# Moving the first spectral piece of a step into the second half of gate and up, and the sigmoids behind the second piece

## The chip, the cores and the metric

The kernel runs on one core of a Trainium2 chip. The metric is the device time of one execution in microseconds (us). The profile is that of one execution; L followed by a number is a source line of the kernel that was profiled.

## The reference

Forward and backward of a gated mix: a spectral branch (2-D FFT, a product with learned weights, inverse FFT) and a GeGLU feed-forward branch. Eight results are wanted: the output and the gradients of everything but `B_x`.

```python
def _A_ref(x, w_r, w_i):
    X = rfft2(x.astype(float32)) * (w_r + 1j * w_i)
    return irfft2(X, s=(S, D)).astype(bfloat16)
def _B_ref(x, w_gate, w_up, w_down):
    return (gelu(x @ w_gate) * (x @ w_up)) @ w_down
g = sigmoid((A_x * gate_w).sum(-1, keepdims=True))
out = g * _A_ref(...) + (1 - g) * _B_ref(...)
# S = 2048 tokens, D = 576, F = 4608; then the vector-Jacobian product with grad_out
```

## The kernel before

After a head of some 51 us there are 72 steps: 18 groups `g` of 256 hidden columns, each with 4 blocks `m` of 512 tokens. I number the steps 0 to 71, so step 37 is g = 9, m = 1. A step computes z (the gradient through w_down) and gate and up for its tokens on TensorE, in two halves of two token tiles; ScalarE takes each half out of PSUM, the memory that the matmuls write (q, xb, hu); VectorE and two sigmoids (om, s) make the tiles A, dHg, dHu. Behind that, TensorE runs weight-gradient units (dwd, dw) of the group before. The FFTs are cut into pieces (pf) and put between these as fillers: in steps 0 to 9 the forward pieces (Y, V), to about step 45 the middle ones (64-partition ones of L659, and L748), then the inverse ones (Z, U, D) to step 64. After the loop come dense matmuls.

The order of a step in the source:

```python
z, xy_full = H_mm(g, m)
xy = xy_full(0)                  # 8 matmuls of 512 columns
da = H_da(m, z)                  # ScalarE empties z
H_act(0, xy, tiles, 0); ...; H_act(0, xy, tiles, 1)     # q, then xb and hu
def second():
    xy = xy_full(1)              # 8 matmuls
    if g == 0:
        fft_next()               # one spectral piece: its matmuls, then its copy by ScalarE
    for part in range(2):
        H_act(1, xy, tiles, part)
    state.append(H_ew1(tiles)); side_work(1.4)
...
second()
at, k, late = 0.0, 0, [sigs]     # at: us of weight-gradient work so far
for w, f in carry + hs:          # halves of dwd (w 1.0) and dw (w 1.7) units
    if k < n and at >= (0.0, 1.0, 3.6, 5.0)[k]:
        fft_next(); k += 1
    if late and at >= 1.6 and k >= min(n, 2):
        late.pop()()             # the sigmoids, then VectorE's eight products
    f(); at += w
```

The PSUM tiles that matter:

```python
ph = tile_pool(name="ph", bufs=2, space=PSUM)    # the two halves of gate and up
pz = tile_pool(name="pz", bufs=1, space=PSUM)    # z AND every spectral piece, one buffer
pw = tile_pool(name="pw", bufs=2, space=PSUM)    # weight gradients (wps), two buffers
```

Each unit's second half ends with its eviction by ScalarE (`wevac`). The units of a group are spread over the blocks: m = 1 has three dwd units (I call it a d step), the other blocks have one or two units of dw, tails or dwd.

## Time and profile before

| | before |
|---|---|
| time, median of 3 | 1480.13 us |
| TensorE busy | 1391.3 us, 94% |
| ScalarE, VectorE busy | 722.1 us (49%), 732.4 us (50%) |
| granted TensorE clock | 0.994 |
| one period of four steps (37 to 40) | 54.08 us |

The period is read between the starts of z. The first and the last of them, from the TensorE timeline of before (columns: start, duration, engine, line, operation, out<-in, shape, count):

```profile
548.08 1.91 PE L380 MATMUL z<-wdT,dOT 128*128 128x256 bf16 x16
...
602.16 1.58 PE L380 MATMUL z<-wdT,dOT 128*128 128x256 bf16 x13
```

602.16 - 548.08 = 54.08. Busy time says little here: a matmul's row is longer than its distance to the next (z: 276 ns on average, 109 ns from start to start). I therefore work with starts: where nothing holds TensorE up, matmuls of 128, 256, 288 and 512 columns start 56, 109, 122 and 216 ns apart in this trace (medians), which N/2.4 + 2.5 ns for N columns fits, and what goes beyond that is lost. Summed this way from the trace, TensorE loses 28.5 us in steps 0 to 9, 49.3 in steps 10 to 44 and 28.6 in steps 45 to 70. Not all of that is waiting: the profiles of before and after lack the record of one gate-and-up matmul per step (1080 of 1152 are there; in experiments 1 to 7 all are), and the sum counts its 0.216 us as lost. Without that it is about 26.3, 41.7 and 23.0 us.

### The profile page before, as it was taken

Reading aid. Unit: us, or ns where it says so; the run is one execution under the profiler, and the core shown is the slowest. Engines: PE = TensorE matmul, PEld = TensorE weight load, DVE = VectorE, ACT = ScalarE, POOL = GpSimd, SP = SyncE. Lnnn points to the kernel's source line nnn. Section 1 sums busy time; section 2 is a strip of 40 time slices with the busy share of each in tenths; the row PEclk is TensorE's granted clock in tenths of the full one; section 3 lists DMA queues with packets and bytes.
Section 4 is the critical chain, followed back from the end, with each engine's and each line's share of the span. In section 5 each row is a group of like instructions: output and inputs, shape, how many; then the busy total and the mean of one; then the engine's idle time right before and its main releaser. Section 6 shows DMA issues by size and latency. Waiting matters only on the chain.

```text
span 1478.9 us, 28110 instructions
## 1 busy us (share of the span) xinstructions
PE 1391.3 (94%) x11342; PEld 1024.0 (69%) x11414; DVE 732.4 (50%) x1394; ACT 722.1 (49%) x1311; POOL 125.7 (8%) x230
## 2 busy tenths in 40 slices
PE   6888898999999999999999999999999999999998
PEld 4555665666666666666676666677877777777776
DVE  6575546767766766755655655653000471212111
ACT  5676777677677677666776666664000000000000
POOL 3000010010010011000001001000000110000000
PEclk9999999999999999999999999999999999999999
DMA  5233354444544543454445436666999997787873
GB/s 187 79 115 106 115 141 122 128 131 128 158 115 117 156 132 112 126 154 113 120 134 158 133 108 153 161 154 144 255 184 189 222 228 162 164 160 163 157 154 75
DMA packets 516477, 214.96 MB, mean 145 GB/s; under 512 B 312921, under 2 KB 510554, under 8 KB 516346
## 3 DMA queue, kind: packets, MB, share of 16 engines
q1 hardware_dynamic: 506714, 192.65, 56.0%
q0 software_dynamic: 7824, 19.49, 4.4%
q8 instruction: 89, 1.46, 0.4%
q10 hardware_dynamic: 1808, 1.02, 0.3%
q14 instruction: 42, 0.34, 0.1%
HBM read 40.76 MB, written 93.84 MB: 91 GB/s over the span
## 4 chain that ended last, share of the span: by engine, by line
PE 80%; ACT 10%; DVE 4%; issue 3%; DMA 1%; SPq 0%; POOL 0%; ACTq 0%; DVEq 0%; POOLq 0%
PE acc L1092 28%; PE xy L392 15%; PE wps L495 12%; PE wps L478 8%; PE z L380 8%; PE wps L508 2%; PE xy L387 2%; ACT hu L412 2%; ACT xb L411 2%; PE z L383 1%; ACT q L409 1%; ACT Vt L751 1%; ACT om L433 1%; ACT Xx L664 1%; ACT Xg L664 1%
## 5 line engine op out<-in xcount | busy, mean ns | idle before, releaser
L1092 PEld LDWEIGHTS <-pin 128*128 128x128 bf16 x3456 | 337.7, 98 | 87.8 <-DMA pin<-scr 2.5
L392 PE MATMUL xy<-wgu,xT 128*128 128x512 bf16 x1080 | 247.6, 379 | 10.2 <-issue 9.5
L495 PEld LDWEIGHTS <-xn 128*128 128x128 bf16 x2304 | 224.3, 98 | 29.6 <-issue 0.2
L392 PEld LDWEIGHTS <-xT 128*128 128x128 bf16 x1152 | 106.8, 98 | 148.8 <-issue 30.6
L402 ACT ACTIVATE da<-z,omg 128x256 bf16<-128x256 f32 x288 | 112.8, 474 | 121.8 <-PE z L383 121.8
L1109 ACT COPY bo<-acc 128x288 f32<-128x288 f32 x32 | 12.7, 398 | 306.8 <-PE acc L1092 282.2
L380 PE MATMUL z<-wdT,dOT 128*128 128x256 bf16 x1152 | 140.6, 276 | 13.5 <-ACT Y L556 5.2
L478 PE MATMUL wps<-dB,A 128*128 128x288 bf16 x1152 | 150.8, 286 | 0.0
L1092 PE MATMUL acc<-wd_all,pin 128*128 128x288 bf16 x1152 | 142.9, 286 | 1.3 <-DMA pin<-scr 1.3
L1092 PE MATMUL acc<-wuT,pin 128*128 128x288 bf16 x1152 | 143.6, 286 | 0.3 <-DMA pin<-scr 0.3
L1092 PE MATMUL acc<-wgT,pin 128*128 128x288 bf16 x1152 | 143.8, 286 | 0.0
L495 PE MATMUL wps<-dHg,xn 128*128 128x256 bf16 x1152 | 136.2, 272 | 0.0
L380 PEld LDWEIGHTS <-dOT 128*128 128x128 bf16 x1152 | 112.9, 99 | 33.5 <-issue 18.3
L438 DVE TENSOR_TENSOR xb<-xb,s 128x1024 bf16<-128x1024 bf16 x72 | 49.8, 692 | 172.7 <-ACT s L434 172.7
L495 PE MATMUL wps<-dHu,xn 128*128 128x256 bf16 x1152 | 134.6, 272 | 0.0
L478 PEld LDWEIGHTS <-A 128*128 128x128 bf16 x1152 | 112.2, 98 | 28.0
L409 ACT ACTIVATE q<-xy 128x512 bf16<-128x512 f32 x144 | 86.0, 597 | 61.0 <-PE xy L392 61.0
L501 POOL DMA_DIRECT2D out_dram<-dw x67 | 48.8, 728 | 658.8 <-ACT dw L456 535.2
L417 DVE TENSOR_SCALAR s<-q 128x1024 bf16<-128x1024 bf16 x72 | 30.7, 426 | 146.0 <-ACT q L409 145.9
L1169 DVE SCALAR_TENSOR_TENSOR f32t<-gwf,dlog,b16t 128x576 f32<-128x576 f32 x16 | 13.1, 818 | 170.6 <-DMA b16t<-dxa_scr 170.6
L412 ACT CAST hu<-xy 128x512 bf16<-128x512 f32 x144 | 87.1, 605 | 0.0
L411 ACT CAST xb<-xy 128x512 bf16<-128x512 f32 x144 | 83.6, 580 | 0.0
(197 smaller groups left out, 1594.5 us busy)
## 6 DMA issues: line engine op xcount, KB each, us to landing
scr<-A SPq DMA_DIRECT2D x72, 256.0 KB, 2.5
scr<-dHg SPq DMA_DIRECT2D x72, 256.0 KB, 2.6
scr<-dHu SPq DMA_DIRECT2D x72, 256.0 KB, 3.0
out_dram<-dw POOLq DMA_DIRECT2D x67, 128.0 KB, 2.3
wd_all<-in_B_w_down_dram SPq DMA_DIRECT2D x3, 1728.0 KB, 14.8
out_dram<-dwd POOLq DMA_DIRECT2D x34, 144.0 KB, 2.8
scr_p<-Vt SPq DMA_DIRECT2D x32, 145.0 KB, 2.4
wgu<-in_B_w_gate_dram SPq DMA_DIRECT2D x18, 256.0 KB, 3.3
```

Source lines behind the costliest of these rows:

```text
L380: nc.tensor.matmul(zo(t), lhsT=dOT[:, ci, t, :], rhs=wdT[:, ci, :], start=(t % 4 < 2 and ci == 0), stop=False)
L392: nc.tensor.matmul(xy[k][:, t % 2, :], lhsT=xT[:, ci, t, :], rhs=wgu[:, ci, :], start=False, stop=(ci == 3))
L402: nc.scalar.activation(da[:, t, :], z[:, t % 2, t // 2, :], ACT.Copy, scale=omg32[:, 4 * m + t:4 * m + t + 1])
L409: nc.scalar.activation(q[:, h, :], xy[:, :, 0:FG], ACT.Square)
L411: nc.scalar.copy(xb[:, h, :], xy[:, :, 0:FG])
L412: nc.scalar.copy(hu[:, h, :], xy[:, :, FG:2 * FG])
L417: V.tensor_scalar(s[:], q[:], A_GELU, 1.0, op0=ALU.mult, op1=ALU.add)
L438: V.tensor_tensor(xb[:], xb[:], s[:], op=ALU.mult)
L478: nc.tensor.matmul(wps[:, :288], lhsT=tl(0, t)[:, fch * P:(fch + 1) * P], rhs=dB[:, t, h * 288:(h + 1) * 288], start=(t == 0), stop=(t == ...
L495: nc.tensor.matmul(wps[:, cc, :], lhsT=xn[:, t, (c0 + cc) * P:(c0 + cc + 1) * P], rhs=tl(k, t), start=(t == 0), stop=(t == T - 1))
L501: wst[0].dma_start(ov[:, c0:c0 + TPB, fsl], dw[:])
L1092: nc.tensor.matmul(acc[:, :288], lhsT=src[:, r, :], rhs=w_of(r)[:, h * 288:(h + 1) * 288], start=(first and r == 0), stop=(last and r == F ...
```

## The change

In the code, `n` is the number of spectral pieces that the schedule gives to a step, `k` how many of them have been placed, and `between` is called in the middle of a half, between its two token tiles. The intent: let the first piece's copy run while TensorE still works on the second half, so that the single pz buffer is free when the second piece comes, and start the sigmoids earlier.

```diff
-        def full(k):
+        def full(k, between=None):
             for t in ts[2 * k:2 * k + 2]:
+                if t % 2 and between:
+                    between()
                 for ci in range(4):
                     nc.tensor.matmul(...)
@@ spectral schedule
-        out = [first] + [gap] * 5
+        out = [first] + [gap] * 7
-    mid_at = 2 * T + 8
+    mid_at = 2 * T + 10
@@ second()
-                xy = xy_full(1)
-                if g == 0:
-                    fft_next()
+                xy = xy_full(1, fft_next if n or g == 0 else None)
@@ the loop over weight-gradient work
-                at, k, late = 0.0, 0, [sigs]
+                at, k, late = 0.0, min(n, 1), [sigs]
-                    if k < n and at >= (0.0, 1.0, 3.6, 5.0)[k]:
+                    if k < n and at >= (0.0, 1.0, 3.0, 5.0)[k]:
-                    if late and at >= 1.6 and k >= min(n, 2):
+                    if late and at >= 1.0:
```

## The prediction

> **What bounds the kernel now.** I read the page first, then who waited for whom on TensorE, then the timelines of TensorE and ScalarE for one period of four steps, because order inside a step is all the change touches.
>
> ```profile
> PE 1391.3 (94%) x11342; PEld 1024.0 (69%) x11414; DVE 732.4 (50%) x1394; ACT 722.1 (49%) x1311; POOL 125.7 (8%) x230
> ```
>
> TensorE is the bound, ScalarE and VectorE are half idle, so only TensorE's gaps can be won. Among its waits the largest are of this kind (columns: waiter, releaser, us in total, times, longest):
>
> ```profile
> PE pf L659 <- ACT Xx L664: 7.6, 8, 1.0
> PE pf L659 <- ACT Vt L751: 6.8, 6, 1.1
> PE pf L748 <- ACT Xg L664: 6.7, 7, 1.0
> ...
> PE z L380 <- ACT ZT L797: 2.2, 2, 1.1
> ```
>
> All spectral pieces (pf) and the step's z use one two-bank PSUM tile, so a piece waits for the copy of the piece before. Now the TensorE timeline from a step with 48 dwd matmuls (call it the d step) into the next:
>
> ```profile
> 554.14 0.41 PE L748 MATMUL pf<-qn,BTtab 128*128 128x290 bf16 x2
> 554.39 1.14 PE L478 MATMUL wps<-dB,A 128*128 128x288 bf16 x8
> 556.67 0.41 PE L659 MATMUL pf<-Vp,Btab 128*128 128x289 bf16 x2 [1.14 <-ACT Vt L751]
> 556.92 5.06 PE L478 MATMUL wps<-dB,A 128*128 128x288 bf16 x40
> 561.82 1.91 PE L380 MATMUL z<-wdT,dOT 128*128 128x256 bf16 x16
> ...
> 567.88 0.41 PE L659 MATMUL pf<-Vp,Btab 128*128 128x289 bf16 x2
> 568.13 1.91 PE L495 MATMUL wps<-dHg,xn 128*128 128x256 bf16 x16
> 570.99 0.41 PE L659 MATMUL pf<-Vp,Btab 128*128 128x289 bf16 x2 [0.95 <-ACT Xx L664]
> ```
>
> and ScalarE in the d step:
>
> ```profile
> 552.61 0.60 ACT L409 ACTIVATE q<-xy 128x512 bf16<-128x512 f32 x1 [0.69 <-PE xy L392]
> ...
> 555.30 0.60 ACT L412 CAST hu<-xy 128x512 bf16<-128x512 f32 x1
> 555.77 0.85 ACT L751 CAST Vt<-pf 128x580 bf16<-128x580 f32 x1
> 557.12 1.28 ACT L664 CAST Xx<-pf 64x578 bf16<-64x578 f32 x2 [0.49 <-PE pf L659]
> 558.42 0.40 ACT L456 CAST dwd<-wps 128x288 bf16<-128x288 f32 x1
> 558.72 1.06 ACT L433 ACTIVATE om<-s 128x1024 bf16<-128x1024 bf16 x1
> 559.81 1.06 ACT L434 ACTIVATE s<-s 128x1024 bf16<-128x1024 bf16 x1
> ```
>
> The first piece's copy stands behind all six copies of gate and up; ScalarE reaches it at 555.77 although its matmuls began at 554.14. The second piece waits it out. Lost time, start to start: 40 dwd matmuls fill 556.92 to 561.82, 0.1225 us each; eight after 554.39 end at 555.37, so the piece at 556.67 is 1.30 late. In the next step 16 matmuls of 256 columns end at 568.13 + 16 x 0.109 = 569.88 (0.109: sixteen z matmuls take 1.91, the last of them 0.27, so 1.64 over 15), so 570.99 is 1.11 late. The period's other two steps lose 1.11 and 0.54 likewise.
>
> **What the Trainium skill says.** "Perfetto Trace Analysis", section Optimization Strategy: a gap that repeats on the engine that should be full can mean that no buffer is free for the next tile. The trace agrees: 1.11 and 1.30 recur every four steps. "TensorE: Matmul & The Clock Gate", section Architectural detail, has ScalarE's queue as strictly first in first out while TensorE may only pull weight loads ahead; the copy at 555.77 behind hu shows the first half. The same page, Back-to-back issue gap, gives columns/2.4 + 2.5 ns, 109 ns for 256, which is what I measure. And "Perfetto Trace Analysis", section Matmuls, wants independent groups to rotate through PSUM banks so evacuation hides; wps has two buffers and does, pf has one and doesn't.
>
> **The change, part by part.** It adds and removes no work. In a step with pieces, the first goes between the two token tiles of the second half, its copy ahead of that half's q, xb, hu; the third piece comes a bit earlier; two empty slots shift the middle stage; the sigmoids follow the second piece at once. The built order of the new kernel confirms this, and shows one more move: in the d step ScalarE had copy, copy, dwd, om, s, dwd, dwd; now it has copy, (q xb hu), copy, om, s, dwd, dwd, dwd. The first dwd eviction has fallen behind both sigmoids.
>
> I write X for the first q of a step (552.61 above), when the second half's matmuls start. Spacings on ScalarE from the trace: q to xb 0.49, xb to hu 0.47, hu to next 0.48; Vt to next 0.70; the pair of Xx copies 1.19; om to s 1.09; s to eviction 0.97. The first piece now runs at X+0.85 and its copy at X+1.44 (hu of the first half starts at X+0.96). The second half ends on TensorE at X+1.96.
>
> *Step with two 64-partition pieces (the one at 566.35).* Copy 1.44 to 2.73, so the second piece, due at 1.96 + 1.745 = 3.70, no longer waits: the 1.11 goes. q 2.63, hu 3.59, second copy 4.14, om 5.33, s 6.42, dw 7.39. TensorE ends with 3.95 + 1.745 + 1.96 = X+7.65, against 8.59 (574.94 - 566.35): gain 0.94. *Next step*: 3.95 + 1.745 + 3.49 = 9.19 against 10.12, gain 0.93. *Next*: 7.65 against 8.01, gain 0.36.
>
> *The d step.* Copy 1.44 to 2.29, q 2.14, hu 3.10, second piece at 2.94 without waiting, its copy 3.58 to 4.87, om 4.77, s 5.86, first dwd 6.83 to 7.23. But dwd units rotate through the two wps buffers, and the third takes the first's buffer. It is due at 2.94 + 0.25 + 24 x 0.1225 = 6.13 and must wait until 7.23 + 0.05 (the release at 556.67 came 0.05 after the copy's end). It ends at 7.28 + 16 x 0.1225 = 9.24, against 9.21 before: the 1.30 is replaced by 1.15 and the gain is nil.
>
> So a period gains 0.94 + 0.93 + 0.36 - 0.03 = 2.20 instead of the 4.06 it loses. There are seven periods in the middle stage (the steps from 208.9 to 602 us, 30 of them): 15.4. At its edges: a third piece put into its first step costs 0.6 at the end but spares 0.25 before it; the d step with one piece now stalls 0.64; the two last steps with four short pieces win back 1.07. Middle: about 15.5.
>
> *Inverse stage (20 steps, 664 to 945 us).* The same reckoning with copies of 1.02 (ZT), 0.37 (ZU), 0.66 (ev). Start-to-start losses at pieces and at z after one are some 14 us. The d steps here go well: one with four pieces has first dwd evicted by 6.5 and the third unit due at 6.7. Where the fourth piece ends a step, z still waits for its copy: 0.6 to 1.3 in six steps, as before, but in other steps. Step by step the sum of gains is 9.2, less 1.8 for three d steps that have no first piece but whose dwd eviction also falls behind the sigmoids (0.56, 0.56, 0.67: third unit due at X+5.55, released at 6.11). Net 7.4.
>
> *Forward stage (first ten steps, 51 to 184 us).* In the first four the piece waits for VectorE, whose Vt sums stand behind the elementwise chain, and now four matmuls of the half queue behind that waiting piece: q comes 0.33 later in three steps, 0.55 earlier in the first. Steps five to ten gain 0.85, 0.71, 0.15, 0.13, -0.2, 0.12. Net 1.3.
>
> Everything after about 1010 us (dense matmuls, 98% busy) is untouched. Sum 15.5 + 7.4 + 1.3 = 24.2 us, 1480.1 - 24.2 = 1456.
>
> **Rivals.** *A, all pf waits vanish and nothing replaces them.* For: ScalarE is 49% busy, and the middle stage loses 32 us start to start (7 x 4.06 and the edges). Then 32 + 9 + 1 = 42 us, 1438, over 2% faster. Against: the dwd eviction order above, and nobody hides a copy that ends a step. *B, the new wps wait is worse than I reckon*, for instance because om also waits for VectorE's s (q delayed by 0.4, then tensor_scalar and product), or because a delayed q makes VectorE late for the A, dHg, dHu tiles. VectorE waits up to 5.9 us for the sigmoids, so it has room; s is ready at X+4.0, before om's turn at 4.77. If every d step lost 1 us more, 17 us of the gain would go: 1473. *C, forward steps become slower*, since a waiting piece in the middle of a half blocks four matmuls (0.86 us) and delays q. At worst 0.5 in four steps: +2 us, and a slip into half clock such as the trace shows at 85 us (z took 3.31 instead of 1.91) may add 1.4.
>
> **Range and chances.** Durations and orders are measured, the addition is mine; the most doubtful are the inverse stage (plus or minus 4) and the d steps (plus or minus 5). Range 1447 to 1468. Over 2% faster means under 1450.5, 6 us beyond my centre: 0.2. Within 2%: 0.78. Slower by over 2%: 0.02.
>
> **What would show it.** Right: waits of pf on Xx, Vt and Xg (some 24 us in the list above with their kin) nearly gone; a new wait of PE wps L480 for ACT dwd, about 1.1 us, in each d step; steps of 12.2, 13.7, 12.2 and 13.8 us in a period instead of 13.1, 14.7, 12.6 and 13.7; busy times unchanged. Wrong: no such wps wait (rival A), waits of the moved piece itself on hu or da, or gaps before z in the middle stage.

## The result

| | before | after |
|---|---|---|
| median of 4 runs | 1478.66 us (1477.17 to 1481.99) | 1459.97 us (1457.31 to 1461.30) |
| profiled span | 1478.9 us | 1457.1 us |

The ratio is 0.9868, with a 95% interval from 0.9843 to 0.9893: 1.3% faster, inside the predicted range of 1447 to 1468 and within 2%.

The page's first line after, then the longest waits of TensorE after (waiter, releaser, us in total, times, longest):

```profile
PE 1386.9 (95%) x11342; PEld 1023.7 (70%) x11414; DVE 731.4 (50%) x1394; ACT 715.5 (49%) x1311; POOL 125.6 (9%) x230
```

```profile
PE wps L480 <- ACT dwd L458: 10.7, 13, 1.3
...
PE pf L568 <- DVE Vt L575: 5.7, 4, 2.0
...
PE pf L661 <- ACT Vt L753: 2.2, 1, 2.2
```

The 24.5 us of middle pieces waiting for copies of Xx, Vt and Xg (7.6, 6.8 and 6.7 in the prediction's list, and 3.4 of L748 for Vt) have shrunk to single cases, and a wait that before did not have has taken the first place: dwd matmuls wait for the eviction of an earlier dwd, 13 times. The third line is one single wait of 2.2 us, to which experiment 6 returns.

The d step after (step 37) and the next one, from the TensorE timeline:

```profile
541.70 0.41 PE L750 MATMUL pf<-qn,BTtab 128*128 128x290 bf16 x2
541.95 1.02 PE L394 MATMUL xy<-wgu,xT 128*128 128x512 bf16 x4
542.81 1.14 PE L480 MATMUL wps<-dB,A 128*128 128x288 bf16 x8
543.79 0.41 PE L661 MATMUL pf<-Vp,Btab 128*128 128x289 bf16 x2
544.04 3.10 PE L480 MATMUL wps<-dB,A 128*128 128x288 bf16 x24
548.41 2.12 PE L480 MATMUL wps<-dB,A 128*128 128x288 bf16 x16 [1.27 <-ACT dwd L458]
...
558.43 0.41 PE L661 MATMUL pf<-Vp,Btab 128*128 128x289 bf16 x2
```

and ScalarE in the same d step:

```profile
541.04 0.60 ACT L411 ACTIVATE q<-xy 128x512 bf16<-128x512 f32 x1 [0.69 <-PE xy L394]
...
542.47 0.85 ACT L753 CAST Vt<-pf 128x580 bf16<-128x580 f32 x1
543.15 0.64 ACT L411 ACTIVATE q<-xy 128x512 bf16<-128x512 f32 x1
...
544.57 1.33 ACT L666 CAST Xx<-pf 64x578 bf16<-64x578 f32 x2
545.80 1.05 ACT L435 ACTIVATE om<-s 128x1024 bf16<-128x1024 bf16 x1
546.89 1.06 ACT L436 ACTIVATE s<-s 128x1024 bf16<-128x1024 bf16 x1
547.97 0.70 ACT L458 CAST dwd<-wps 128x288 bf16<-128x288 f32 x2
```

The first piece stands between two groups of gate-and-up matmuls, and its copy (542.47) ahead of the second q (543.15). Neither this d step's second piece (543.79) nor the next step's (558.43) waits any more. But the first dwd eviction now follows om and s. It starts at 547.97; the third dwd unit, which needs its buffer, could have started at 544.04 + 24 x 0.1225 = 546.98 and starts at 548.41, 1.43 late.

Lengths of steps 37 to 40, between the starts of z:

| step | before | predicted | after | experiment 1 |
|---|---|---|---|---|
| 37 (d step) | 13.74 | 13.77 | 13.87 | 12.44 |
| 38 | 13.13 | 12.18 | 12.01 | 12.01 |
| 39 | 14.67 | 13.72 | 13.56 | 13.56 |
| 40 | 12.55 | 12.18 | 12.02 | 12.01 |

The predicted column is the end of each step after X, as the prediction has it, plus 4.53 us from z to X (552.61 - 548.08). Over the whole kernel, by stages between starts of z:

| stretch | before | after | gain | predicted |
|---|---|---|---|---|
| head, to step 0 | 50.8 | 49.8 | 0.9 | 0 |
| steps 0 to 9 | 133.3 | 135.5 | -2.2 | 1.3 |
| steps 10 to 44 | 468.4 | 452.9 | 15.6 | 15.5 |
| steps 45 to 70 | 352.5 | 345.3 | 7.2 | 7.4 |
| rest | 474.0 | 473.6 | 0.3 | 0 |

The change does not touch the head, so its 0.9 shows how far two executions scatter.

### The profile page after: what moved, and what is told of

The parts are those of the page before. It is cut to its first block, busy times and chain, and to the rows that moved or that the text cites. A ratio compares the mean times of both kernels' runs of the same rounds, so it can differ in the third digit from the quotient of the medians.

```text
span 1457.1 us, 28112 instructions
## 1 busy us (share of the span) xinstructions
PE 1386.9 (95%) x11342; PEld 1023.7 (70%) x11414; DVE 731.4 (50%) x1394; ACT 715.5 (49%) x1311; POOL 125.6 (9%) x230
## 3 DMA queue, kind: packets, MB, share of 16 engines
q10 hardware_dynamic: 1808, 1.02, 0.2%
## 4 chain that ended last, share of the span: by engine, by line
PE 82%; ACT 9%; DVE 3%; issue 3%; SPq 1%; DMA 1%; POOL 0%; ACTq 0%; DVEq 0%; POOLq 0%
PE acc L1092 28%; PE wps L497 16%; PE xy L394 14%; PE z L380 8%; PE wps L480 7%; PE xy L387 2%; PE wps L510 2%; PE z L383 1%; ACT om L435 1%; ACT xb L413 1%; ACT hu L414 1%; ACT q L411 1%; DMA pin<-scr 1%; ACT Xx L666 1%; ACT s L436 1%
## 5 line engine op out<-in xcount | busy, mean ns | idle before, releaser
L394 PE MATMUL xy<-wgu,xT 128*128 128x512 bf16 x1080 | 258.8, 380 | 10.1 <-issue 9.4
L480 PE MATMUL wps<-dB,A 128*128 128x288 bf16 x1152 | 153.8, 288 | 10.7 <-ACT dwd L458 10.7
L440 DVE TENSOR_TENSOR xb<-xb,s 128x1024 bf16<-128x1024 bf16 x72 | 49.8, 692 | 108.4 <-ACT s L436 108.4
```

Of the source, the lines that this page charges most:

```text
L394: nc.tensor.matmul(xy[k][:, t % 2, :], lhsT=xT[:, ci, t, :], rhs=wgu[:, ci, :], start=False, stop=(ci == 3))
L440: V.tensor_tensor(xb[:], xb[:], s[:], op=ALU.mult)
L480: nc.tensor.matmul(wps[:, :288], lhsT=tl(0, t)[:, fch * P:(fch + 1) * P], rhs=dB[:, t, h * 288:(h + 1) * 288], start=(t == 0), stop=(t == ...
```

## The experiments

Theory T, after reading this: the moved copy removes the waits of the second piece; the sigmoids' new condition has a cost of its own, the new wps wait in d steps; and in the first four steps a piece that waits for VectorE now blocks half of the gate-and-up matmuls behind it. Its rivals are given with each run. Experiments 1 to 4 ran on one chip and share seven runs of before (median 1482.12 us); 5 to 7 ran together and share nine (1482.94 us).

**1. Sigmoids back to their old condition.**

```diff
-                    if late and at >= 1.0:
+                    if late and at >= 1.6 and k >= min(n, 2):
```

> The changed kernel, only the sigmoids put back to their old condition (from 1.6 us of weight-gradient work on). The built order differs from the changed kernel's in the d steps alone: the first dwd eviction is again ahead of om and s. Theory T (the new wps wait of the d steps comes from that eviction standing behind both sigmoids): the jumps between wps matmuls, 13.0 us in total in the trace of the changed kernel, vanish, a d step of the middle stage goes from 13.87 to about 12.45 us, and the time is 1447 +- 2 us, ratio to before 0.979. Rival R1 (the eviction is late because the moved piece delays q, xb, hu and the second copy, whatever the sigmoids do): the waits stay above 0.5 us each and the time stays above 1455. Rival R2 (the sigmoids need the early place, else VectorE and the next step suffer): the wps wait goes, but other waits of TensorE take its place and the time stays near 1460.

Measured: 1448.51 us (1444.72 to 1450.23), ratio 0.976 (0.9736 to 0.9784). TensorE and then ScalarE in the d step (step 37):

```profile
535.02 0.41 PE L661 MATMUL pf<-Vp,Btab 128*128 128x289 bf16 x2
535.27 5.06 PE L480 MATMUL wps<-dB,A 128*128 128x288 bf16 x40
```

```profile
537.15 0.40 ACT L458 CAST dwd<-wps 128x288 bf16<-128x288 f32 x1
537.45 1.06 ACT L435 ACTIVATE om<-s 128x1024 bf16<-128x1024 bf16 x1
```

The eviction is ahead of om again, the 40 dwd matmuls run through, and no wps wait is left on the list. The sigmoids start 0.30 us later for it and nothing else in the period changes: steps 38 to 40 keep their lengths to 0.01 us. T stands; R1 and R2 fall. Of the changed kernel's parts the sigmoids' move was a loss: about 13 us of jumps between dwd matmuls in its trace, in 13 d steps, set against the gain of the others.

**2. The sigmoids' move alone, on the kernel before.**

```diff
-                    if late and at >= 1.6 and k >= min(n, 2):
+                    if late and at >= 1.0 and k >= min(n, 2):
```

> The kernel before, with nothing changed but the sigmoids' condition (from 1.0 us on), so right behind the second piece. T: alone it only does harm: the first piece's wait of 1.30 us in a d step stays and a wps wait of 0.6 to 0.8 us comes on top in some 14 d steps, so 1479 + 9 = 1488 us (1484 to 1491). Rival (early sigmoids are a gain of their own, through an earlier VectorE): 1479 or less.

Measured: 1494.70 us (1487.83 to 1496.80), ratio 1.0067 (1.0036 to 1.0098). From its waits of TensorE:

```profile
PE wps L478 <- ACT dwd L456: 8.8, 12, 0.9
...
PE pf L659 <- ACT Vt L751: 6.8, 6, 1.1
```

Both waits stand side by side, the old one at its old size. In the trace the loop is 11.5 us longer; d steps of the middle stage go from 13.74 to 14.80. So the harm is more than expected (1.06 per d step where I had said 0.6 to 0.8), the time lies outside the 1484 to 1491 that I had given, and the sign is as T had it.

**3. The old order in the first four steps.**

```diff
-                xy = xy_full(1, fft_next if n or g == 0 else None)
+                xy = xy_full(1, fft_next if n and g > 0 else None)
+                if g == 0:
+                    fft_next()
```

> The changed kernel, but in the first four steps the piece is put behind the whole half again, as before. T: there the piece waits for VectorE, and four matmuls of the half and then q queue behind it; so steps 1 to 3 fall from 12.61, 11.66, 11.66 to about 11.2 us each, and step 0 gets 0.3 to 0.5 longer: 1.5 to 2 us less, 1458. Rival (these steps are bound by the VectorE chain in either order): their lengths do not change, 1460.

Measured: 1457.99 us (1456.33 to 1460.24), ratio 0.983 (0.9804 to 0.9855). That range overlaps the changed kernel's, which ran in other rounds, so the time alone decides nothing; the step lengths do. Steps 1 to 3 went from 12.61, 11.66, 11.66 to 11.17, 11.17, 11.20 us, step 0 from 10.26 to 10.56. The first V of step 1 in the changed kernel, then in this one:

```profile
68.20 0.51 PE L568 MATMUL pf<-Y,Rt 128*128 128x290 bf16 x2 [2.00 <-DVE Vt L575]
68.50 1.91 PE L394 MATMUL xy<-wgu,xT 128*128 128x512 bf16 x4
```

```profile
68.64 0.42 PE L568 MATMUL pf<-Y,Rt 128*128 128x290 bf16 x2 [1.14 <-DVE Vt L575]
```

V is released by VectorE; asking for it 0.86 us earlier only makes it wait 0.86 us longer, with four gate-and-up matmuls behind it. In this trace these took 1.91 instead of the 1.02 of other steps, so half a clock came on top in step 1. T stands by its step lengths.

**4. Only the copy ahead, the piece's matmuls behind the whole half.**

```diff
-                xy = xy_full(1, fft_next if n or g == 0 else None)
+                xy = xy_full(1)
+                if n or g == 0:
+                    fft_next()
```

> The changed kernel, but the first piece's matmuls come behind the whole half, and only its copy stays ahead of that half's q, xb, hu. Theory C (what counts is the copy's place in ScalarE's queue, not the place of the matmuls): the copy starts at X+2.15 instead of X+1.44 and ends by X+3.4, in time for the second piece at X+3.7, so the steps without dwd wait keep their 12.0, 13.6, 12.0 us; the d steps get up to 0.7 longer (second copy, om and s all move), the first four steps are those of before (-2): in sum 1463 us (1459 to 1467). Rival (the matmuls must be inside the half): waits of pf for copies of 0.5 us and more return in the middle stage, 1470 or more.

Measured: 1467.62 us (1466.50 to 1469.25), ratio 0.9893 (0.9872 to 0.9914), just outside what I had expected. Steps 38 to 40 are 12.02, 13.56, 12.02 us: the same as with the piece inside the half. The d step is 14.40 instead of 13.87, with

```profile
549.97 2.12 PE L480 MATMUL wps<-dB,A 128*128 128x288 bf16 x16 [1.72 <-ACT dwd L458]
```

So in the steps with two middle pieces the place of the copy in ScalarE's queue is what removes the wait, and the place of the matmuls doesn't matter there. It matters where ScalarE is on the path: q, om, s and the dwd eviction all come later (copy at 544.04, X+1.97 after q at 542.07, where the change has X+1.43). With the sigmoids back in their old place this should cost less; I did not run that.

**5. Both repairs (1 and 3).** The edits are those two diffs together.

> The changed kernel with both repairs: sigmoids at their old condition, and in the first four steps the piece behind the whole half. T: the two repairs touch different steps, so their gains add: about 13 us and about 2 us less than the changed kernel, ratio to before 0.975 (0.972 to 0.978), over 2% faster than before. Rival (they share a bound, for instance the granted clock of the first steps): no better than the sigmoids' repair alone, 0.976 or more in the ratio and the same lengths of the first four steps as there.

Measured: 1444.39 us (1441.17 to 1444.91), ratio 0.9733 (0.9713 to 0.9753). Over 2% faster than before. Steps 1 to 3 are 11.18, 11.42, 11.13 and the middle d steps 12.44: each repair has its effect where it had it alone.

**6. Also the store of Vt ahead of the loads.** Step 21 of the changed kernel was 16.64 us long where its kin had 13.87, and no prediction of mine had that. In experiment 5 it was still 16.99. ScalarE, then SyncE's queue there:

```profile
329.30 0.81 ACT L753 CAST Vt<-pf 128x580 bf16<-128x580 f32 x1 [3.22 <-DMA scr_p<-Vt]
```

```profile
318.59 0.41 SPq L626 DMA_DIRECT2D Vp<-scr_x  x1
...
319.70 2.78 SPq L652 DMA_DIRECT2D Wt<-in_A_w_r_dram  x6
322.53 3.60 SPq L652 DMA_DIRECT2D Wt<-in_A_w_i_dram  x6
326.23 0.90 SPq L755 DMA_DIRECT2D scr_p<-Vt  x2
```

The copy writes one of two Vt buffers and has to wait until the store that reads it has landed; that store stands in SyncE's queue behind fourteen loads for a later pair, which the same piece had issued first. In step 20 those loads in turn stood behind twelve stores. In the kernel before, the twelve stores came after the corresponding store (331.73 against 330.73), and step 21 had no such wait. The edit, on top of experiment 5:

```diff
             def f():
-                if key == "m1" and b == 1 and p + 2 < T // 2:
-                    prefetch(p + 2)
                 ...
                 LD.dma_start(dst[g:g + 2]..., Vt[:])
+                if key == "m1" and b == 1 and p + 2 < T // 2:
+                    prefetch(p + 2)
```

> As e5_both, and the loads of the pair after next are issued behind the store of Vt instead of ahead of it. Theory S: the single wait of 2.3 to 3.1 us in step 21 (a copy into Vt waits for the store that last read that buffer, and this store stands behind fourteen loads in SyncE's queue) goes, so step 21 is 12.4 us as its kin and the time is 3 us less than that of e5_both. Rival (the store would be late anyway, its data or the DMA engines being the limit): step 21 keeps 2 us or more of wait.

Measured: 1440.17 us (1437.45 to 1441.68), ratio 0.9707 (0.9687 to 0.9727), the best of all: 2.9% faster than before and ahead of the changed kernel. Step 21 is 12.44 us and the wait is gone. That is 4.55 us less, more than the 3 us I had expected: in experiment 5 the 40 dwd matmuls behind the wait also took 6.73 us instead of the 5.06 of other d steps, at a granted clock of 0.76 (330 to 337 us). SyncE's queue now has the store first:

```profile
320.80 0.38 SPq L753 DMA_DIRECT2D scr_p<-Vt  x1
321.28 0.41 SPq L626 DMA_DIRECT2D Vp<-scr_x  x1
```

The start-to-start losses are now 24.4, 12.8 and 13.3 us in the three stretches where before had 26.3, 41.7 and 23.0 (without its missing records).

**7. The move alone.** The kernel before with the piece in the half from step 4 on, and neither the shift by two slots, nor the earlier third piece, nor the sigmoids.

```diff
-                xy = xy_full(1)
+                xy = xy_full(1, fft_next if n and g > 0 else None)
...
-                at, k, late = 0.0, 0, [sigs]
+                at, k, late = 0.0, min(n, 1), [sigs]
```

(with `between` in `full` as in the change)

> The kernel before with nothing but the move of the first piece into the half (not in the first four steps): no shift by two slots, the third piece from 3.6, sigmoids from 1.6. T: the shift only moved a third piece into step 12, where its copy stands behind the sigmoids and z waits 1.76 us; so without it step 12 is about 12 us instead of 14.2, step 11 is 0.25 longer, and the time is 1 to 2 us less than that of e5_both. Rival (the shift by two slots is needed, since the middle stage otherwise starts before its data have landed): new waits for DMA in steps 11 to 13, 2 us and more slower than e5_both.

Measured: 1447.37 us (1447.16 to 1449.14), ratio 0.976 (0.9742 to 0.9779). Here T is wrong in its sign: I expected 1 to 2 us less than experiment 5, and the median is 3 us more. Both signs of the rival came: a new wait for DMA, and over 2 us. Step 12 did fall from 14.16 to 12.01, as said. But step 13 rose from 13.68 to 15.47, at its second piece:

```profile
228.58 0.41 PE L661 MATMUL pf<-Vp,Btab 128*128 128x289 bf16 x2 [2.88 <-DMA Vp<-scr_x]
```

It waits for data (Vp) whose load is issued only when SyncE's queue comes to it, and that moment does not move (173.0 us after the start of step 0 in experiment 5, 173.1 here), so the time saved in step 12 is spent waiting in step 13 (3.04 us lost at that piece, 1.24 in experiment 5). In steps 43 to 64 pieces fall into other places; in both kernels six of them end a step, and they hold z by 5.95 us in total here and by 5.23 in experiment 5. Over the loop the trace is 1.2 us longer than that of experiment 5. The rest of the 3 us lies before and behind the loop, where the two kernels have the same instructions: the head was 1.4 us longer in this profile, at a granted clock of 0.93 against 0.97, and the part behind the loop 1.8. I take it for scatter, but all five runs here lie above all four of experiment 5, so its cause is not shown. So the move of one piece is 35.6 us of medians by itself. The shift and the earlier third piece, which experiment 5 has and this one has not, are worth about a microsecond together in the loop; no run takes them apart. The sigmoids' move is a loss (experiments 1 and 2).

## Why the prediction was right

- **What bounds it, and what the move removes: right.** The waits of middle pieces are gone. The gain in the steps with two pieces was mis-sized, 0.94, 0.93 and 0.36 where the trace has 1.11, 1.11 and 0.54. The term that failed is "X (552.61 above), when the second half's matmuls start". X is ScalarE's first q, and TensorE starts the second half before that: the piece ran at 541.70, X+0.66, where I had X+0.85. All of TensorE's times after X were 0.19 too late, and the second piece's wait vanished completely.
- **The d step: right in mechanism and nearly in size.** "the 1.30 is replaced by 1.15" became 1.43. Of the difference of 0.28, 0.19 is the same offset (the third unit was due at X+5.94, not 6.13) and 0.09 is the release (X+7.37, not 7.28: from s to the eviction it was 1.08, where I had taken 0.97 from a step whose first eviction was already done). The d step lost 0.13 instead of 0.03. Experiment 1 proves the cause by taking it away.
- **Middle stage: 15.5 foretold, 15.6 measured, and two errors of about equal size hide in it.** The larger gain per period (1.11 + 1.11 + 0.54 - 0.13 = 2.63 instead of 2.20) would have made it some 3 us better; step 21, with its wait for the store of Vt, took 2.8 back (16.64 against 13.87). The prediction had no term for that; experiment 6 shows its cause. That the sum of the stage came out to 0.1 us is luck.
- **Inverse stage and end: 7.4 foretold, 7.2 measured.** The d steps without a first piece lost 0.65, 0.65 and 0.69 at their third unit where I had 0.56, 0.56 and 0.67. Two d steps with first pieces, which the prediction has "go well", lost 0.36 and 0.35 there (steps 53 and 61). Pieces that end a step still hold z, by 0.62 to 1.26 in six steps.
- **Forward stage: wrong, 1.3 foretold, -2.2 measured.** Rival C, "forward steps become slower", is what happened. Steps 1 to 3 lost 1.43, 0.49 and 0.44, not 0.33 each. Step 4 lost 0.72 where I had "0.85" of gain: om waited 1.69 us for VectorE (0.61 before), so the third piece's copy behind the sigmoids was late and z waited. VectorE is full there in both kernels, since it also scales eight tiles of dB (2.31 us). What is new is its order: the two Vt sums of the moved piece (105.47 and 105.84) now stand ahead of the s that om needs (106.21), where before they came after it, and they take 0.74 from start to start. I had counted ScalarE's queue there and forgotten VectorE's. The wait is the same with the sigmoids in their old place (1.69 in experiment 1), so it belongs to the piece's move. The rest is granted clock, which does not belong to the change: step 0 was lucky (z took 3.48 us in the profile of before; at full clock the old order takes 10.56 for the step, experiment 3, not 12.13) and step 7 unlucky (fifteen z matmuls took 3.36 us; 12.85 us in experiments 1, 3, 5 and 7 with the same order, 15.68 here).
- **Rival A fell, as it was argued to.** Its 1438 needs the sigmoids' new place undone, and then comes close: 1444.39 in experiment 5.
- **The sum.** 24.2 us foretold, 21.8 between the profiled spans, 18.7 between the medians; the profiled run of the changed kernel was one of its two faster ones. The forward stage alone, 3.5 us off, is larger than the net errors of all other stretches together.

## What to carry to other kernels

When one PSUM buffer is shared by a chain of small pieces, the place of each copy in the evacuating engine's queue decides whether the next piece waits; moving one piece, and its copy with it, ahead of work that is not urgent was worth 2.4% here (experiment 7). Before moving a block of long instructions forward on such an engine, list every eviction that it overtakes and ask which buffer that eviction frees and when it is next needed: two sigmoids of 1.06 us ahead of one eviction of 0.40 us cost about 13 us in 13 places. Ask the same of every other engine on which the moved work leaves instructions: here two sums of 0.45 us on VectorE came ahead of the tile that the sigmoids needed, and one step lost 0.72. And a piece that waits for another engine should not be put in front of matmuls that wait for nobody.

## What the Trainium skill lacked or had wrong

- "Perfetto Trace Analysis", Optimization Strategy, says that a repeating gap can mean too little room for the next tile, and names buffer count and tile sizes. The gaps here were of that kind, but were removed without another buffer, by the order of copies on ScalarE (experiments 1 and 7: 1.11 and 1.30 us per step to none). The section's general advice, to make a dependency start sooner, covers this; it does not name the order of evacuations in an engine's queue as a way to do it.
- "DMA: Bandwidth & Descriptors" describes how descriptors complete, but gives no figure measured on trn2 for how long SyncE is held per DMA; its table on trn3 has 512 cycles per copy under "previous generations". Here fourteen loads held SyncE for 7.5 us, 0.54 us each (318.59 to 326.13, experiment 5), and a store behind them made ScalarE wait 3.22 us.
